# One weight load of a decode kernel, w1, sent as two transfers: 16 rows, then 112

## The chip, the cores and the metric

The kernel runs on one core of a Trainium2 chip. The metric is the device time of one execution in microseconds (us); lower is better. Before the change it is 342.52 us, the median of three runs (342.45 to 342.62).

## What is computed

Two rows x (batch 2, one token each, 512 wide) pass through two branches, mixed by a gate. The reference, cut to what matters:

```python
g = sigmoid((x * gate_w).sum(-1, keepdims=True))
# branch A: attention over a cache, 32 heads of 128, 4096 positions
q = (x @ wq).reshape(2, 1, 32, 128).transpose(0, 2, 1, 3)
p = softmax(einsum("bhqd,bhkd->bhqk", q, k_cache) * 128 ** -0.5)
a = einsum("bhqk,bhkd->bhqd", p, v_cache).transpose(0, 2, 1, 3).reshape(2, 1, 4096) @ wo
# branch B: two dense layers, 512 -> 1376 -> 512
b = maximum(x @ w1, 0) @ w2
out = g * a + (1 - g) * b
```

All tensors are bf16. k_cache and v_cache hold 67 MB each; the weights together some 11 MB. Nearly all that the kernel does is to bring these bytes on chip once.

## The kernel before

On-chip memory has 128 partitions. One large tile, `kv`, holds three regions of 8 MB (NREG = 3, 64 KB on each partition). The k and v caches are cut into eight units of 8 MB each (NU = 8). SyncE (SP) issues one transfer for a unit, into the region that is next in turn; the list `order` fixes the sequence of k and v units by hand. From the fourth unit on, SP first waits until the work on the unit that had the region before has ended (`freed`), so up to three units are in flight or in use.

The third region first serves another end: it holds wq (4 MB), w1 (1.4 MB), x and gate_w, since these are needed only at the start. ScalarE (ACT) issues the loads of x (L233) and gate_w (L234) on its own queue. SP issues w1 (L235) and then wq (L236), then the first two k units (L250). The third k unit needs the region of the weights, and SP waits there for `pe_qh`, `dve_setup` and `act_q`: the projections must have read wq and w1, and q must have been taken out.

On TensorE (PE), `gate()` turns x and forms the gate's sum. Then `x_proj()` forms q (from wq) and the first dense layer (from w1) in one loop of four passes; its matmuls go through the helpers on L314 and L320. Ahead of it PE waits for wq and for w1. A transfer of SP adds 16 to its semaphore when it has landed, so the wait is for 16 on each.

w1 is 512 x 1376. The load views it as 128 rows of four consecutive lines (`"(p t) f -> p (t f)"`), so a partition gets 4 x 1376 x 2 = 11,008 consecutive bytes. There are sixteen DMA engines, and a transfer's rows are dealt out among them.

From there on the units stream: VectorE (DVE) turns each k unit in place (L404), PE multiplies (L314), ACT and DVE form the softmax, GpSimd (POOL) spreads the weights p (L449), and PE multiplies the v units. At the end SP loads w2 (L252) and wo in four pieces (L255); the last matmuls (L598) add both branches into one result, two casts (L623, L625) write it out, and SP sends it (L257).

The instructions of each engine are collected in a list and emitted in two parts: a first few of each (the tuple `rest`; for SP the first four: w1, wq and two k units) ahead of PE's program, the others behind it.

Of the kernel before, what the change touches and what calls it, by code (L numbers as in the profile page):

```python
# [94 lines left out]
def bass_gated_mix__gqa_block_cached__dense_activation_relu__decode_kernel(  # L95
# [61 lines left out]
    w1_sb = kv[:, C, 16384:21888]  # L157
# [16 lines left out]
    def psf(p0, p1, c0, n):  # L174
        return PSF[p0:p1, c0:c0 + n]
# [4 lines left out]
    sem = {n: nc.alloc_semaphore("sem_" + n) for n in names}  # L180
# [16 lines left out]
    def freed(what):  # L197
        kind, u = what
        return f"pesc_{u}" if kind == "k" else f"pe_v_{u}"

    def sp(fn, waits=(), dwaits=()):
        P.add("sp", fn, waits=waits, dwaits=dwaits)
# [4 lines left out]
    def dve(fn, waits=(), signal=None, dwaits=()):  # L207
        P.add("dve", fn, waits=waits, signal=signal, dwaits=dwaits)

    def act(fn, waits=(), signal=None, dwaits=()):  # L210
        P.add("act", fn, waits=waits, signal=signal, dwaits=dwaits)

    def pe(fn, waits=(), signal=None, dwaits=()):
        P.add("pe", fn, waits=waits, signal=signal, dwaits=dwaits)
# [17 lines left out]

    act(lambda e: e.dma_start(x_sb[0:2], A_x.rearrange("b s d -> (b s) d")).then_inc(sem["x"], 16))  # L233
    act(lambda e: e.dma_start(x_sb[2:3], gate_w.rearrange("(o d) -> o d", o=1)).then_inc(sem["gw"], 16))  # L234
    sp(lambda e: e.dma_start(w1_sb, B_w1.rearrange("(p t) f -> p (t f)", t=4)).then_inc(sem["w1"], 16))  # L235
    sp(lambda e: e.dma_start(wq_sb, A_wq.rearrange("(p t) n -> p (t n)", t=4)).then_inc(sem["wq"], 16))  # L236
    for n, what in enumerate(order):
        if n >= NREG:
            waits = [freed(order[n - NREG])]
        else:  # L240
            waits = ["pe_qh", "dve_setup", "act_q"] if n == C else []
        if what == ("v", 7):
            c0 = 0
            for i, k in enumerate(LASTV):
                c1 = c0 + k * 4096
                sp(lambda e, n=n, c0=c0, c1=c1, i=i: e.dma_start(kv[:, n % NREG, c0:c1], unit_in(("v", 7))[:, c0:c1]).then_inc(sem["v7" + "ab"[i]], 16),
                   waits=waits if i == 0 else [])
                c0 = c1
        else:
            sp(lambda e, n=n, what=what: e.dma_start(kv[:, n % NREG, :], unit_in(what)).then_inc(sem_reg[n % NREG], 16),  # L250
               waits=waits)
# [50 lines left out]
    def r_(e, name):  # L302
        if name not in reg:
            reg[name] = e.alloc_register(name)
        return reg[name]

    def by_reg(e, ap, name):
        x = e.lower_ap(ap)
        n = reg[name].name
        return mybir.RegisterAccessPattern(ap=x.ap, dtype=x.dtype, memsetref=x.memsetref, regref=n, is_regloc_offset=False,  # L310
                                           reg_ap_offset=n, const_ap_offset=0, const_sub_tensor_id=0)

    def mm(e, dst, lhsT, rhs, cols=128, at=0, load=True):
        return e.add_instruction(mybir.InstMatmult(  # L314
            name=nc.get_next_instruction_name(), engine=mybir.EngineType.PE, ins=[rhs, lhsT], outs=[e.lower_ap(dst)],
            start_tensor_calc=False, stop_tensor_calc=False, tile_size=(128, cols), tile_position=(0, at),
            bass_skip_group_check=True, ldweights=load))

    def clear(e, dst, n, stop=False):
        return e.matmul(dst, lhsT=nil, rhs=nil.unsqueeze(1).to_broadcast([32, 4, 128]) if n == 512 else nil[:, 0:n],  # L320
                        start=not stop, stop=stop, tile_position=(0, 0), skip_group_check=True)

    def addresses(e, base, offs, first):
        for k, o in enumerate(offs):
            e.reg_add(r_(e, f"a{first + k}"), r_(e, base), o)
# [4 lines left out]
    def enter(name, parent=None, engines=(mybir.EngineType.PE,)):  # L330
        parent = nc.bb_map[parent] if parent else nc.cur_bb
        if open_block:
            open_block.pop().__exit__(None, None, None)
        b = nc.body(name, parent=parent, valid_engines=list(engines))
        b.__enter__()
        open_block.append(b)
# [3 lines left out]
    def x_proj():  # L340
        wqv = wq_sb.rearrange("p (t u a x) -> p t a u x", t=4, u=4, a=4)
        place_of = [(96 + r, 10, 128) for r in range(10)] + [(0, 1, 96)]

        def fn(e):
            for half in range(2):
                clear(e, psf(0, 128, V_C0 + BANK * half, BANK), 512)
            clear(e, psf(0, 128, H_C0, 2 * NF), 2 * NF)
            e.reg_mov(r_(e, "rm"), at["kv"] + 2 * C * REG)
            e.reg_mov(r_(e, "rh"), at["kv"] + 2 * (C * REG + 16384))
            e.reg_mov(r_(e, "rw"), at["zero"] + 4 * 636)  # L350
            e.reg_mov(r_(e, "p"), 0)
            e.br("x_pass")
            enter("x_pass")
            addresses(e, "rm", [2 * (256 * a + 2048 * half) for a in range(4) for half in range(2)], 0)
            addresses(e, "rw", [2 * 31], 8)
            addresses(e, "rh", [2 * (row + (m - 1) * n) for row, n, m in place_of], 9)
            for a in range(4):
                for half in range(2):
                    mm(e, psf(32 * a, 32 * a + 32, V_C0 + BANK * half, BANK), by_reg(e, xT32[:, 0, :], "a8"),
                       by_reg(e, wqv[:, 0, a, 2 * half:2 * half + 2, :], f"a{2 * a + half}"), 32, 32 * a, load=not half)  # L360
            for ft, (row, n, m) in enumerate(place_of):
                mm(e, psf(0, m, H_C0 + 2 * ft, 2), by_reg(e, w1_sb[:, row:row + (m - 1) * n + 1:n], f"a{9 + ft}"),
                   by_reg(e, xT32[:, 0, 0:2], "rw"))
            e.reg_add(reg["rm"], reg["rm"], 2 * 4096)
            e.reg_add(reg["rh"], reg["rh"], 2 * DFF)
            e.reg_add(reg["rw"], reg["rw"], 2 * 32)
            e.reg_add(reg["p"], reg["p"], 1)
            e.br_lt(reg["p"], 4, on_true="x_pass", on_false="x_done")
            enter("x_done")
            return clear(e, psf(0, 128, H_C0, 2), 2, stop=True)  # L370
        pe(fn, dwaits=[(sem["wq"], 16), (sem["w1"], 16)], waits=["act_xT"], signal="pe_qh")
        qt = ptm[:].rearrange("p x c h -> p (x c h)").bitcast(f32)
        dve(lambda v: v.transpose(out=qt.rearrange("p (n q) -> p n q", q=32).rearrange("p (y e) q -> p y e q", e=2),  # L373
                                  in_=PSF[:, V_C0:V_C0 + 1024].rearrange("p (y q e) -> p y e q", q=32, e=2)),
            waits=["pe_qh"], signal="dve_qt")
        act(lambda a: a.activation(out=q_sb[:].rearrange("p b u h k -> p b (u h k)"),
                                   in_=qt.rearrange("p (n x) -> p x n", x=32)[:, 0:2], func=ACT.Copy),
            waits=["dve_qt"], signal="act_q")
# [265 lines left out]
    hint_here()  # L644
    gate()
    x_proj()
    w_block(0)
    w_block(1)
# [48 lines left out]

    P.resolve()

    rest = (("sp", nc.sync, 4), ("act", nc.scalar, 2), ("pool", nc.gpsimd, 4), ("dve", nc.vector, 0))  # L700
    for name, eng, n in rest:
        P.emit(name, eng, 0, n)
    P.emit("pe", nc.tensor)
# [31 lines left out]
```

## Time and profile before

| what | value |
|---|---|
| median of three runs | 342.52 us (342.45 to 342.62) |
| the profiled execution | 342.64 us, of which its span is 341.3 us |
| busy: PE, DVE, POOL, ACT | 209.9, 155.4, 41.8, 13.9 us |
| SP's queue q1: packets, bytes, share of 16 engines | 3460, 145.33 MB, 98.7% |
| mean rate of all transfers | 426 GB/s |
| w1, issue to landing | 1376 KB, 5.8 us |
| wq, issue to landing | 4096 KB, 15.0 us |

The span runs from the first to the last instruction of one profiled execution. A queue's share is the time that its packets took, over sixteen engines and the whole span. A packet is one consecutive piece that one DMA engine moves; for w1 it is one row of 11,008 bytes. In the timeline, a line gives the start, the time, the engine, the source line and the operation; "SPq" and "ACTq" are the instructions by which SP and ACT issue transfers. In the windows, a row gives a stretch, its length, the busy time of PE, PEld (weight loads), DVE, ACT and POOL, then the granted TensorE clock, the DMA share and the rate.

### The profile page before, as it was taken

The numbers are of one execution on the slowest core, as the hardware profiler recorded it, in microseconds if no ns is written. First come the engines' busy times: TensorE is split into PE (matmuls) and PEld (weight loads), VectorE is DVE, ScalarE is ACT, GpSimd is POOL, SyncE is SP. The second block draws the span as 40 slices with busy tenths as digits, with TensorE's granted clock in tenths as the row PEclk, the third lists the DMA queues.
The fourth block names the chain that finished last, engine by engine and source line by source line (L and its number), as shares of the span: only waits on it lengthen the run. The fifth ranks groups of instructions, "written<-read, shape, count | busy, mean of one in ns | idle before, by whom it ended". The sixth has DMA issues, their size and how long they took to land. (4 is left out here: it accounts for less than half of the span.)

```text
span 341.3 us, 3101 instructions
## 1 busy us (share of the span) xinstructions
PE 209.9 (61%) x1243; PEld 33.9 (10%) x843; DVE 155.4 (46%) x45; ACT 13.9 (4%) x37; POOL 41.8 (12%) x53
## 2 busy tenths in 40 slices
PE   0080079685968909972995059820993773718387
PEld 0040011000100101110111001100100100101024
DVE  1010897979799769229800693019805000000111
ACT  2001000000000020000000000000003000000000
POOL 1000000000000004005002300050000235050400
PEclk9999999999898965996799559965696659676789
DMA  8998989898999999998989898989999999999896
GB/s 346 434 492 369 492 369 492 369 492 369 492 392 468 399 461 445 415 484 376 492 369 492 369 492 369 492 369 492 392 468 392 468 438 424 398 441 461 374 440 264
DMA packets 3580, 145.46 MB, mean 426 GB/s; under 512 B 405, under 2 KB 634, under 8 KB 762
## 3 DMA queue, kind: packets, MB, share of 16 engines
q1 hardware_dynamic: 3460, 145.33, 98.7%
q10 hardware_dynamic: 118, 0.10, 0.1%
q8 instruction: 1, 0.02, 0.0%
q14 instruction: 1, 0.01, 0.0%
HBM read 145.43 MB, written 0.00 MB: 426 GB/s over the span
## 5 line engine op out<-in xcount | busy, mean ns | idle before, releaser
L404 DVE STREAM_TRANSPOSE kv<-kv 128x8192 uint32<-128x8192 uint32 (+1 forms) x17 | 138.6, 8186 | 74.4 <-DMA kv<-in_A_k_cache_dram 74.4
L314 PE MATMUL PS<-kv,zero 128*128 (+1 forms) x544 | 130.3, 421 | 40.4 <-PEq L481 40.4
L314 PE MATMUL PS<-kv,ptw 128*32 x512 | 48.1, 469 | 11.7 <-issue 11.5
L320 PE MATMUL PS<-zero 32*128 32x512 bf16 (+2 forms) x21 | 9.7, 537 | 57.6 <-ACT zero L410 20.3
L449 POOL TENSOR_TENSOR ptw<-E,mask 128x512 bf16<-128x512 bf16 x32 | 32.2, 1038 | 21.1 <-PE PS L314 10.9
L467 DVE TENSOR_TENSOR X<-PS,maskc 128x512 f32<-128x512 f32 x2 | 1.4, 692 | 64.1 <-PE PS L314 64.1
L314 PEld LDWEIGHTS PS<-kv,zero 128*128 (+1 forms) x144 | 13.6, 103 | 154.6 <-issue 154.6
L393 POOL TENSOR_TENSOR zero<-q_sb,mask 128x32 bf16<-128x32 bf16 x8 | 1.9, 251 | 147.0 <-PE PS L314 123.3
L471 POOL TENSOR_TENSOR X<-X,maskc 128x512 f32<-128x512 f32 x6 | 6.2, 1039 | 109.2 <-ACT X L470 109.2
L314 PE MATMUL PS<-X,zero 128*64 128x512 f32 x16 | 11.6, 819 | 12.3 <-PEq L481 12.3
L314 PEld LDWEIGHTS PS<-kv,ptw 128*32 x512 | 8.7, 99 | 50.4 <-issue 49.7
L320 PEld LDWEIGHTS PS<-zero 32*128 32x128 bf16 x21 | 2.1, 109 | 69.4 <-issue 43.7
L373 DVE STREAM_TRANSPOSE ptw<-PS 128x1024 f32<-128x1024 f32 x1 | 1.3, 1251 | 16.4 <-PE PS L320 16.4
L415 DVE TENSOR_REDUCE zero<-PS 128x2 f32<-128x2048 f32 x2 | 4.5, 2271 | 9.1 <-PE PS L314 9.1
L470 ACT ACTIVATE X<-PS 128x512 f32<-128x512 f32 x6 | 3.6, 597 | 71.4 <-PE PS L314 71.4
L422 ACT ACTIVATE nrow<-mmax 128x32 f32<-128x32 f32 x2 | 0.5, 228 | 132.8 <-DVE mmax L419 132.8
L440 DVE STREAM_TRANSPOSE E<-E 128x2048 bf16<-128x2048 bf16 x2 | 4.6, 2300 | 2.4 <-ACT E L430 2.4
L410 ACT ACTIVATE zero<-zero 1x1 f32<-1x1 f32 x9 | 1.8, 200 | 84.9 <-DMA kv<-in_A_v_cache_dram 67.9
L430 ACT ACTIVATE E<-PS,negm 128x1024 bf16<-128x1024 f32 x4 | 4.4, 1109 | 0.6 <-DVE negm L426 0.6
L284 PE MATMUL PS<-kv 3*128 3x3 bf16 x4 | 0.3, 165 | 6.5 <-DMA kv<-in_gate_w_dram 6.5
L598 PE MATMUL PS<-kv,oW 128*2 128x256 bf16 x64 | 4.0, 272 | 0.4 <-DMA kv<-in_A_wo_dram 0.4
L314 PEld LDWEIGHTS PS<-X,zero 128*64 (+1 forms) x16 | 1.8, 161 | 15.8 <-issue 15.6
(49 smaller groups left out, 27.6 us busy)
## 6 DMA issues: line engine op xcount, KB each, us to landing
kv<-in_A_v_cache_dram SPq DMA_DIRECT2D x1, 6144.0 KB, 36.7
kv<-in_A_wq_dram SPq DMA_DIRECT2D x1, 4096.0 KB, 15.0
kv<-in_A_wo_dram SPq DMA_DIRECT2D x1, 2560.0 KB, 35.9
kv<-in_A_v_cache_dram SPq DMA_DIRECT2D x1, 2048.0 KB, 41.3
kv<-in_B_w_dram SPq DMA_DIRECT2D x1, 1376.0 KB, 5.8
kv<-in_B_w_dram SPq DMA_DIRECT2D x1, 1280.0 KB, 30.1
kv<-in_A_wo_dram SPq DMA_DIRECT2D x1, 1024.0 KB, 37.9
kv<-in_A_wo_dram SPq DMA_DIRECT2D x1, 384.0 KB, 38.4
```

Source lines behind the costliest of these rows:

```text
L314: return e.add_instruction(mybir.InstMatmult(name=nc.get_next_instruction_name(), engine=mybir.EngineType.PE, ins=[rhs, lhsT], outs=[e.low ...
L320: return e.matmul(dst, lhsT=nil, rhs=nil.unsqueeze(1).to_broadcast([32, 4, 128]) if n == 512 else nil[:, 0:n], start=not stop, stop=stop, ...
L393: pool(lambda g: g.tensor_tensor(out=out, in0=q, in1=msk, op=ALU.mult), waits=([["act_q", "dve_mask8"], []] + [[f"pesc_{x}"] for x in rang ...
L404: ins = v.transpose(out=reg[:, 4096 * p0:4096 * p1], in_=reg[:, 4096 * p0:4096 * p1])
L410: return lambda a: a.activation(out=tick[:, 2 + i:3 + i], in_=tick[:, 0:1], func=ACT.Copy).then_inc(sem["go"], n)
L415: dve(lambda v: v.tensor_reduce(out=mpad[:, 0:2], in_=PSF[:, 0:2048].rearrange("p (x h q) -> p h x q", h=2, q=16), axis=AX.XY, op=ALU.max) ...
L430: act(lambda a, h=h: a.activation(out=E[:].rearrange("p (x h q) -> p h x q", h=2, q=16)[:, h], in_=PSF[:, 0:2048].rearrange("p (x h q) -> ...
L440: dve(lambda v: v.transpose(out=E[:], in_=E[:]), waits=[f"act_exp{b}"], signal=f"dve_et{b}")
L449: pool(lambda g, src=src, dst=dst: g.tensor_tensor(out=dst, in0=src, in1=msk, op=ALU.mult), waits=(([f"dve_et{b}"] if ub == 0 else []) + ( ...
L470: act(lambda e: e.activation(out=X2[:], in_=src, func=ACT.Copy), waits=[f"pe_v_{v}"], signal=f"act_x_{v}")
L471: pool(lambda e: e.tensor_tensor(out=X, in0=X, in1=msk, op=ALU.mult).then_inc(sem["xg"], 1), waits=[f"act_x_{v}"] + ([] if v else ["dve_se ...
L598: pe(lambda e, g=g: e.matmul(psf(64 * g, 64 * g + 2, FIN_C0, 256), lhsT=w, rhs=m[:, 256 * g:256 * g + 256], start=start, stop=stop, tile_p ...
```

## The change

w1 is loaded by two transfers on the same queue: the first sixteen rows (partitions 0 to 15), then rows 16 to 127. Both add 16 to the same semaphore, and PE waits for 32. SP's first part of the program has five instructions instead of four. Nothing else differs.

```diff
-    sp(lambda e: e.dma_start(w1_sb, B_w1.rearrange("(p t) f -> p (t f)", t=4)).then_inc(sem["w1"], 16))
+
+    for p0, p1 in ((0, 16), (16, 128)):
+        sp(lambda e, p0=p0, p1=p1: e.dma_start(w1_sb[p0:p1], B_w1.rearrange("(p t) f -> p (t f)", t=4)[p0:p1]).then_inc(sem["w1"], 16))
     sp(lambda e: e.dma_start(wq_sb, A_wq.rearrange("(p t) n -> p (t n)", t=4)).then_inc(sem["wq"], 16))
...
-        pe(fn, dwaits=[(sem["wq"], 16), (sem["w1"], 16)], waits=["act_xT"], signal="pe_qh")
+        pe(fn, dwaits=[(sem["wq"], 16), (sem["w1"], 32)], waits=["act_xT"], signal="pe_qh")
...
-    rest = (("sp", nc.sync, 4), ("act", nc.scalar, 2), ("pool", nc.gpsimd, 4), ("dve", nc.vector, 0))
+    rest = (("sp", nc.sync, 5), ("act", nc.scalar, 2), ("pool", nc.gpsimd, 4), ("dve", nc.vector, 0))
```

## The prediction

> **What bounds the kernel now.** I read the busy shares first, then the DMA queues, then the chain that ended last, and then the first microseconds in small windows. The page's second and third parts:
>
> ```profile
> DMA  8998989898999999998989898989999999999896
> GB/s 346 434 492 369 492 369 492 369 492 369 492 392 468 399 461 445 415 484 376 492 369 492 369 492 369 492 369 492 392 468 392 468 438 424 398 441 461 374 440 264
> ...
> q1 hardware_dynamic: 3460, 145.33, 98.7%
> ```
>
> No compute engine passes 61% (PE, 209.9 us of 341.3); SP's queue q1 keeps sixteen DMA engines occupied for 98.7% of the span. Nothing in the middle is slack: 145.33 MB in 0.987 x 341.3 = 336.9 us is 431 GB/s, and every slice stands near it except the first (346) and the last (264). So **the end is where the DMA stream ends**, and a shift of the stream's start moves the end by as much, undiminished. The end itself, from the timeline:
>
> ```profile
> 339.05 0.37 PEld L598 LDWEIGHTS PS<-kv,oW 128*2 128x2 bf16 x8 [0.28 <-DMA kv<-in_A_wo_dram]
> 339.69 0.38 ACT L625 ACTIVATE ptw<-PS 2x256 bf16<-2x256 f32 x1 [5.21 <-PE PS L598]
> 339.69 0.41 DVE L623 CAST ptw<-PS 2x256 bf16<-2x256 f32 x1 [5.82 <-PE PS L598]
> 340.13 0.33 SPq L257 DMA_DIRECT2D out_dram<-ptw  x1
> ```
>
> The last matmuls wait for the last pieces of wo, and only the casts and the 2 KB output follow. The slowest of the sixteen engines decides, since each landing needs all of them.
>
> The change sits at the other end. The timeline of the first 3 us, then the windows (length, five engines' busy time, granted clock, DMA share, GB/s):
>
> ```profile
> 0.74 0.40 SPq L235 DMA_DIRECT2D kv<-in_B_w_dram  x1
> 0.74 0.54 ACTq L233 DMA_DIRECT2D kv<-in_A_x_dram  x1
> ...
> 1.19 0.42 SPq L236 DMA_DIRECT2D kv<-in_A_wq_dram  x1
> 1.31 0.23 ACTq L234 DMA_DIRECT2D kv<-in_gate_w_dram  x1
> ...
> 1.65 1.16 SPq L250 DMA_DIRECT2D kv<-in_A_k_cache_dram  x2
> ```
> ```profile
> 1.00:1.50 0.50, 0.00 (x0) 0.00 (x0) 0.00 (x0) 0.00 (x0) 0.33 (x2) 1.00 0.00 0
> 1.50:2.00 0.50, 0.00 (x0) 0.00 (x0) 0.00 (x0) 0.00 (x0) 0.50 (x1) 1.00 1.16 180
> 2.00:2.50 0.50, 0.00 (x0) 0.00 (x0) 0.08 (x1) 0.03 (x1) 0.39 (x1) 1.00 0.61 154
> 2.50:3.00 0.50, 0.00 (x0) 0.00 (x0) 0.50 (x4) 0.50 (x1) 0.00 (x0) 1.00 0.34 132
> 3.00:3.50 0.50, 0.00 (x0) 0.00 (x0) 0.50 (x3) 0.50 (x1) 0.00 (x0) 1.00 1.14 484
> ```
>
> w1 is issued at 0.74 us; nothing moves before 1.5; then for 1.5 us the stream runs at 132 to 180 GB/s before it reaches its rate. The windows book a packet's bytes where it starts. The packet records behind these rows say the same: w1 is 128 packets of 11,008 bytes, eight to an engine. The first packet of each engine starts between 1.77 and 2.73 us and takes 0.41 to 1.36 us, 0.92 on the mean; the later ones take 0.413 us (26.65 GB/s an engine). This **ramp** is what the change touches.
>
> **The change part by part.**
>
> *It removes* nothing: same bytes, same packets.
>
> *It adds* one DMA instruction on SP, and turns the first transfer into sixteen rows (16 x 11,008 = 176 KB, one packet an engine) and the second into 112 rows (seven an engine). That a few rows do go one to an engine is seen on x, whose two rows are two overlapping packets of 1,024 bytes.
>
> (a) *An earlier first byte.* x (two rows, ACT's queue) and w1 (128 rows) are both issued at 0.74; x's packets start at 1.67, w1's first at 1.77: a shorter transfer starts 0.10 us earlier. The output's two rows are issued at 340.13 and start at 340.89, 0.76 us later, against 1.03 us for w1: 0.27 earlier. Nothing excludes zero. Bounds 0 to -0.27; I take **-0.10**, the pair issued at the same moment.
>
> (b) *A later second transfer.* SP's steps in the timeline are 0.74, 1.19, 1.65: one instruction more costs 0.45 us. So seven eighths of w1 become available 0.45 us later, while the first packet feeds an engine for 0.41 us. Balance **+0.04**. If SP's added step were as short as the output's issue (0.33, and the same 0.05 between), it would be 0.38 and the balance -0.03. wq and the k regions are issued 0.45 later as well, which costs nothing: w1 still occupies the engines until about 6.5 us (0.74 + its 5.8 to landing), 4.8 us after k's first issue at 1.65. If that cover were gone, it would cost the whole 0.45.
>
> (c) *Sixteen neighbouring rows at once.* In the trace every long transfer spreads sixteen engines over all 128 partitions. The new first transfer aims all sixteen at partitions 0 to 15. No row shows that. The one near row is x: two engines writing partitions 0 and 1 at the same time took 44 ns each, against 46 for a packet of that size elsewhere, so no sharing; but that is 2 KB, little enough to be taken up on the way, and not 176 KB. If n engines share a way into neighbouring partitions, a packet takes n x 0.413: bounds n = 1 (cost 0, x's pair) and n = 16 (cost 6.2). I take the geometric middle, n = 4: 1.65 instead of 0.41, **+1.24**. A hidden part would need idle DMA time behind it, and the page has none. [...]
>
> (d) *112 rows in sevens.* 128 rows run at 0.413 us a packet; sevens that begin at row 16 need not keep the engines apart as eights do. Bounds 0 (w1's own rate) and +2.89 (each of seven packets at double time). I take **0**, the nearest row, and keep the upper end for the range.
>
> *It moves* PE's wait on w1 from a count of 16 to 32. PE waits there for wq too, issued at 1.19 with 15.0 us to landing, so about 16.2; the first matmul of x_proj starts at 16.28, when w1 has been there nearly 10 us. Queued behind that wait is all of PE's projection, and behind it q and the issue of the third k region, at 26.4; but the two regions issued before it still fill the engines for 16.8 MB / 426 GB/s = 39 us after 16. Cost 0.
>
> **Sum:** -0.10 + 0.04 + 1.24 + 0 = **+1.18 us**. The profiled execution took 342.64 us, its span 341.3 and 1.3 around it; it would become 343.8. That run is 0.12 above the median of three, 342.52, so the forecast is **343.7 us**.
>
> **The rivals.**
>
> *Nothing moves.* If x's pair is the right row for (c), -0.10 + 0.04 = -0.06: **342.5**. For it: the step (0.45) and the packet (0.41) are almost equal, so the first transfer only fills the time until the second arrives. Against: it needs sixteen writers side by side to run as freely as two. [...]
>
> *The ramp goes away: faster.* From 1.67 (x's first packet) to 3.5 the windows book 0.5 x (180 + 154 + 132 + 484) = 475 KB; at 427 GB/s it would be 781 KB. The missing 306 KB are 0.72 us. If the ramp is the price of preparing eight packets an engine before any flows, and the short transfer escapes it as x's did, with the second ready in time, the gain is 0.72 + 0.10: **341.7**. With the larger lead it is 0.99, 341.5. For it: x shows no slow packet. Against: (b), the second transfer comes 0.45 us later and would show its own ramp.
>
> *The ramp is paid twice: slower, by another way.* An engine with one packet has nothing queued behind it; if the second transfer starts cold again, its first packet costs 0.92 instead of 0.41 on the mean, 1.36 on the worst engine: +0.51 to +0.95. With (a) and (b), +0.45 to +0.89, middle **343.2**. It decides from the point where the first packet ends before the second transfer's packets are ready. Against: if the first packet is itself slow, the second start is hidden behind it.
>
> That the change does not do what it says (the sixteen rows on fewer than sixteen engines) would put several packets in a row on some engines; four each is the same 1.24 late on those, so its time is the forecast's, and I count it there.
>
> **How the numbers follow.** Neighbouring rows share a way: 0.38, 343.2 to 344.9 (n = 3, +0.77, up to n = 4 with a part of (d)). Ramp twice: 0.12. Nothing moves: 0.30, 342.2 to 342.9. Ramp gone: 0.20, 341.5 to 342.2. A measurement of this kernel tells about 0.2%, 0.69 us, from no change: slower holds nearly all of the first case and most of the second, 0.46; faster holds most of the last, 0.17; the rest, 0.37, is within. For eight in ten the range reaches from the middle of the faster case to the first case's upper end, 341.8 to 344.9, and leaves out half of the faster case and the part of (c) and (d) above n = 4.
>
> **What would show it.** In the packet records, w1's first sixteen packets: about 1.65 us each, or several ends in steps of 0.41, bears (c) out; 0.41 from 1.7 on refutes it. The packets of the 112 rows at 0.413 bear out (d); longer ones among them would price it. First packets of the second transfer near 0.92 mean the second ramp. The issue of wq should move from 1.19 to about 1.64, the first matmul of x_proj (16.28) and the last wo landing (339.05) by the same amount as the end. If the windows after 4 us show a rate other than now, or the first matmul moves and the end does not, the view that the stream carries its start to the end is wrong, and with it every step here.

## The result and the profile after

The changed kernel takes 344.71 us (median of six runs, 344.51 to 345.35) against 342.57 for the kernel before beside it (342.45 to 342.74): 2.14 us slower, ratio 1.0063, 95% interval 1.0052 to 1.0074. The forecast was 343.7 with a range of 341.8 to 344.9. The sign held; the loss is 1.8 times the forecast's 1.18 us, and the larger part of it comes from a term that the sum had put at nothing.

The page after, its second and third parts:

```profile
DMA  7999898989899998989898999989898989899896
GB/s 226 451 466 474 382 481 374 489 367 489 367 489 397 458 474 382 489 367 489 367 489 367 489 412 443 481 374 489 367 489 367 489 367 491 372 462 458 370 437 265
...
q1 hardware_dynamic: 3476, 145.33, 98.7%
```

The share is the same 98.7%, though less was moved per microsecond (145.33 MB in a span of 343.2 us instead of 341.3): an engine that is held up in a packet counts as occupied. The sixteen packets more are of 4 bytes each (402 of that size instead of 386), and the kernel has one transfer more; w1 itself is still 128 packets of 11,008 bytes. The first slice fell from 346 to 226 GB/s; that is the place of the loss. The timeline's start, SP's issues alone:

```profile
0.74 0.85 SPq L237 DMA_DIRECT2D kv<-in_B_w_dram  x2
1.64 0.49 SPq L238 DMA_DIRECT2D kv<-in_A_wq_dram  x1
2.16 1.00 SPq L252 DMA_DIRECT2D kv<-in_A_k_cache_dram  x2
```

wq is issued at 1.64 instead of 1.19, as foreseen. The same windows as before, and on to 7 us (the columns are as above; the last three are the granted clock, the DMA share and GB/s):

```profile
1.50:2.00 0.50, 0.00 (x0) 0.00 (x0) 0.00 (x0) 0.00 (x0) 0.50 (x1) 1.00 1.05 310
2.00:2.50 0.50, 0.00 (x0) 0.00 (x0) 0.08 (x1) 0.03 (x1) 0.39 (x1) 1.00 0.57 114
2.50:3.00 0.50, 0.00 (x0) 0.00 (x0) 0.50 (x4) 0.50 (x1) 0.00 (x0) 1.00 1.58 264
3.00:3.50 0.50, 0.00 (x0) 0.00 (x0) 0.50 (x3) 0.50 (x1) 0.00 (x0) 1.00 0.38 88
...
4.00:5.00 1.00, 0.40 (x8) 0.23 (x6) 0.00 (x0) 0.44 (x3) 0.00 (x0) 1.00 1.06 330
5.00:6.00 1.00, 0.00 (x0) 0.00 (x0) 0.17 (x1) 0.33 (x2) 0.00 (x0) 1.00 1.09 308
6.00:7.00 1.00, 0.00 (x0) 0.00 (x0) 0.00 (x0) 0.00 (x0) 0.00 (x0) 1.00 0.95 253
```

The kernel before has, from 4 us:

```profile
4.00:5.00 1.00, 0.00 (x0) 0.00 (x0) 0.00 (x0) 0.00 (x0) 0.00 (x0) 1.00 0.91 385
5.00:6.00 1.00, 0.00 (x0) 0.00 (x0) 0.00 (x0) 0.00 (x0) 0.00 (x0) 1.00 1.49 637
6.00:7.00 1.00, 0.26 (x4) 0.20 (x4) 0.00 (x0) 0.17 (x1) 0.00 (x0) 1.00 0.69 295
```

More packets start before 2.0 (310 against 180), so the first transfer does get moving sooner. But where the kernel before books 385, 637 and 295 between 4 and 7 us, 439 on the mean (the 637 holds the first large packets of wq, booked where they start), this one books 330, 308 and 253, 297 on the mean, with the DMA share near 1: the engines are occupied and slow. The packet records show it packet by packet. Mean time of w1's packets, in sets of sixteen in the order of their start, and of wq's first sixteen behind them (us):

```
            w1, 11,008 bytes each                            wq first
before      0.91 0.42 0.41 0.41 0.41 0.42 0.42 0.41          1.21
after       0.59 1.03 0.62 0.59 0.55 0.61 0.69 0.63          1.44
```

The end moved with it. The changed kernel's timeline:

```profile
18.30 1.02 PE L322 MATMUL PS<-zero 32*128 32x512 bf16 x3 [13.62 <-DMA kv<-in_A_wq_dram]
...
340.94 0.37 PEld L600 LDWEIGHTS PS<-kv,oW 128*2 128x2 bf16 x8 [0.25 <-DMA kv<-in_A_wo_dram]
...
342.02 0.32 SPq L259 DMA_DIRECT2D out_dram<-ptw  x1
```

The last wait for wo ends 1.89 us later (339.05 to 340.94), as does the output's issue (340.13 to 342.02); the first matmul of x_proj moved from 16.28 to 18.30, by 2.02; the profiled executions differ by 344.51 - 342.64 = 1.87. What is lost in the first eight microseconds reaches the end whole, within 0.2 us.

### The profile page after: what moved, and what is told of

The parts are those of the page before. It is cut to its first block, busy times and chain, and to the rows that moved or that the text cites. A ratio compares the mean times of both kernels' runs of the same rounds, so it can differ in the third digit from the quotient of the medians.

```text
span 343.2 us, 3102 instructions
## 1 busy us (share of the span) xinstructions
PE 211.0 (61%) x1243; PEld 33.9 (10%) x843; DVE 155.4 (45%) x45; ACT 13.9 (4%) x37; POOL 41.8 (12%) x53
## 3 DMA queue, kind: packets, MB, share of 16 engines
q1 hardware_dynamic: 3476, 145.33, 98.7%
## 5 line engine op out<-in xcount | busy, mean ns | idle before, releaser
L316 PE MATMUL PS<-kv,zero 128*128 (+1 forms) x544 | 131.9, 425 | 39.2 <-PEq L483 39.2
L316 PEld LDWEIGHTS PS<-zero,kv 128*128 (+1 forms) x44 | 3.0, 158 | 3.5 <-issue 3.5
L316 PE MATMUL PS<-zero,kv 128*128 (+1 forms) x44 | 3.3, 200 | 0.0
```

What stands on the lines that cost most here:

```text
L316: return e.add_instruction(mybir.InstMatmult(name=nc.get_next_instruction_name(), engine=mybir.EngineType.PE, ins=[rhs, lhsT], outs=[e.low ...
```

## The experiments

Theory A: engines meet at the destination. Each DMA engine writes a share of the rows, and when a transfer does not cover all 128 partitions, several engines would write through the same way (entrance) into on-chip memory and wait for each other; it would hold for the 112 rows above all. A way is an assumption: it is not seen in any record, only what rows cost that are thought to share one. Theory B: two transfers would cost more than one, by a second cold start. Theory C is A for the sixteen rows: sixteen neighbouring rows would share ways by fours, the four being the forecast's estimate. Each kernel starts from the kernel before; differences are between medians of runs made side by side. The cuts of code show the load alone; the counts that PE waits for, and SP's first part of the program, follow it.

**e1: both transfers with all 128 rows, split by columns.**

```diff
+    for c0, c1 in ((0, 688), (688, 5504)):
+        sp(... e.dma_start(w1_sb[:, c0:c1], B_w1.rearrange("(p t) f -> p (t f)", t=4)[:, c0:c1]) ...)
```

> w1 in two transfers of all 128 rows each: the first 1,376 bytes of every row (176 KB, as much as the sixteen rows held), then the other 9,632. If the loss comes from how 112 rows are dealt to the engines (theory A), it is gone: between 0.3 us faster and 0.3 slower than the kernel before, with packets of 9,632 bytes at about 0.36 us. If it comes from sending two transfers, with a second cold start (theory B), the second transfer's first packets are again about 0.6 us too long and the time is 0.6 to 1.9 us above the kernel before.

342.80 against 342.69, ratio 1.0006 (0.9997 to 1.0016): no difference. The packets of 9,632 bytes run at 0.36 us, and its windows show the full rate between 4 and 6 us:

```profile
4.00:5.00 1.00, 0.27 (x4) 0.18 (x4) 0.17 (x1) 0.43 (x3) 0.00 (x0) 1.00 0.98 414
5.00:6.00 1.00, 0.00 (x0) 0.00 (x0) 0.00 (x0) 0.15 (x1) 0.00 (x0) 1.00 1.05 441
```

So the second transfer, SP's added issue and a slow second start (the first sixteen of its large packets take 0.80 us on the mean, 0.36 being full rate) cost together nothing that these runs can tell from zero (-0.10 to +0.55 us). B, which asked for 0.6 at least, falls. The small first transfer brings no gain either. Why the slow second start costs nothing is not shown; that it falls into time which the stream loses at its start anyway would fit.

**e2: 112 rows first, then sixteen.**

```diff
+    for p0, p1 in ((16, 128), (0, 16)):
```

> Rows 16 to 127 first, rows 0 to 15 behind them. Theory A (sevens): the 112 packets after the first of each engine stay at 0.55 to 0.69 us instead of 0.41 although nothing stands ahead of them, and the time is 1.5 to 2.2 us above the kernel before. Theory B (second cold start): the 112 packets run at 0.41, the sixteen show the slow start, at most 0.6 us above. Theory C (sixteen neighbouring rows share a way): the sixteen packets take about 1.65 us each and cost 1.2.

345.76 against 342.69, 3.07 us slower (1.0086, 1.0069 to 1.0103): more than any one theory said, and what A (1.5 to 2.2) and C (1.2) come to together. After their slow start the packets of the 112 rows keep to means of 0.50 to 0.71 us, as A has it with nothing ahead of them. The packets of about 1.65 us that C foretold do not show: the last sixteen of w1 take 0.82. But wq's first packets behind them take 2.11 us instead of 1.21. The two excesses, 0.41 and 0.90, make 1.31 us, near the price of C; I read the second as the same writes, booked one packet later. Here, in mid-stream, the whole price shows.

**e3: two halves.**

```diff
+    for p0, p1 in ((0, 64), (64, 128)):
```

> Rows 0 to 63, then 64 to 127: four rows an engine. Theory A in the form 'engines meet when the rows a transfer covers are fewer than all 128': packets at up to 0.83 us, 3.3 us above the kernel before at most; in the form 'only odd shares such as sevens make them meet': 0.41 us and no loss. Theory B: 0.6 us above.

345.75 against 342.69, 3.06 us slower (1.0086, 1.0069 to 1.0102). Its packets settle at 0.85 us, twice 0.413, and the stream at half rate:

```profile
4.00:5.00 1.00, 0.00 (x0) 0.00 (x0) 0.00 (x0) 0.00 (x0) 0.00 (x0) 1.00 0.97 199
5.00:6.00 1.00, 0.00 (x0) 0.00 (x0) 0.00 (x0) 0.00 (x0) 0.00 (x0) 1.00 1.09 253
6.00:7.00 1.00, 0.32 (x6) 0.27 (x6) 0.00 (x0) 0.19 (x1) 0.00 (x0) 1.00 1.10 231
7.00:8.00 1.00, 0.22 (x4) 0.13 (x4) 0.17 (x1) 0.48 (x3) 0.00 (x0) 1.00 0.91 187
```

In this run half of the partitions gave about half of the rate (187 to 253 GB/s from 4 to 8 us, where e1 has 414 and 441 from 4 to 6), with even shares (four rows an engine) too.

**e4: sixteen rows once more ahead of the whole w1**, into spare bytes of the same region (`spare`, behind x's columns of `kv`).

```diff
+    sp(... e.dma_start(spare[0:16], B_w1.rearrange("(p t) f -> p (t f)", t=4)[0:16]) ...)
     sp(... w1 as before ...)
```

> The kernel before, with rows 0 to 15 of w1 read once more ahead of it, into spare bytes of partitions 0 to 15; w1 itself stays whole, and PE waits for both. This adds one packet an engine, 0.41 us at full rate. If the narrow transfer costs nothing beyond its bytes, 0.3 to 0.5 us above the kernel before. If sixteen neighbouring rows share ways by fours (theory C), its bytes need 1.65 us, part of which passes while the stream would only be starting: 1.0 to 1.7 us above, and the packets behind it, not its own, are long.

343.74 against 342.62, 1.12 us slower (1.0032, 1.0022 to 1.0042). The added bytes are worth 0.41, so the narrow transfer costs about 0.7 at the head of the stream, not 1.24. The 0.7 is a middle and no level that was measured: the ten runs fall in two groups of five, at 343.4 and at 344.0 to 344.4, with the median between them, and the interval gives 0.3 to 1.0. That the missing part is hidden in the start is argued, not shown. The packets behind it are long, not its own (0.53, then 1.05), as C has it; a second slow start would look alike here, and only e1 says that it costs no more than 0.55.

**e5: 112 rows once more behind w1**, with e10, all 128 rows at the same place, as control, and e11 with rows 32 to 127.

```diff
     sp(... w1 as before ...)
+    sp(... e.dma_start(spare[16:128], B_w1.rearrange("(p t) f -> p (t f)", t=4)[16:128]) ...)
```

> The kernel before, with a transfer of rows 16 to 127 of w1 once more, into spare bytes of the same region, behind w1 and ahead of wq; PE waits for it too. This adds 7 packets an engine in the middle of a running stream. Theory A: packets at about 0.62 us, so 4.3 us more than the kernel before, and up to 0.3 on top from the first packets behind it. Theory B: no cold start in a running stream, packets at 0.413, 2.9 us more.

> Control for the added 112 rows: all 128 rows of w1 once more into the spare bytes. At full rate 8 packets of 0.413, 3.3 us above the kernel before, less than the 4.2 that 112 rows cost, though it moves more.

> Rows 32 to 127 once more into the spare bytes, six an engine. At full rate 2.5 us above the kernel before. If any share other than eight makes engines meet, 3.3 to 4.5; if only odd shares do, 2.5.

| added rows | bytes at full rate | measured | ratio and interval |
|---|---|---|---|
| 128 (e10) | 8 x 0.413 = 3.30 us | +3.29 (345.88 against 342.59) | 1.0095 (1.0078 to 1.0112) |
| 112 (e5) | 7 x 0.413 = 2.89 us | +4.24 (346.93 against 342.69) | 1.0130 (1.0113 to 1.0147) |
| 96 (e11) | 6 x 0.413 = 2.48 us | +4.85 (347.44 against 342.59) | 1.0142 (1.0125 to 1.0158) |

In these runs fewer rows than 128 took longer. The control meets its bytes to 0.01 us; 112 rows lose 1.35 and 96 lose 2.37, with a time of 4.85 beyond the 4.5 that I had put as the upper end. That only odd shares do it is refuted: sixes lose too. Whether 96 rows take longer than 112 the times do not settle, since their intervals overlap; the packets of the added 96 rows do take longer, 0.68 to 0.75 us in the sets behind the first against 0.52 to 0.64. The windows from 7 us, e10 first, then e11:

```profile
7.00:8.00 1.00, 0.27 (x4) 0.18 (x4) 0.11 (x1) 0.47 (x3) 0.00 (x0) 1.00 0.88 374
8.00:9.00 1.00, 0.00 (x0) 0.00 (x0) 0.05 (x1) 0.20 (x1) 0.00 (x0) 1.00 1.24 528
```
```profile
7.00:8.00 1.00, 0.50 (x8) 0.33 (x8) 0.00 (x0) 0.36 (x2) 0.00 (x0) 1.00 0.98 242
8.00:9.00 1.00, 0.00 (x0) 0.00 (x0) 0.17 (x1) 0.41 (x2) 0.00 (x0) 1.00 1.17 275
```

A DMA share near 1 at 242 GB/s: again occupied and slow.

**e6: w1 in eight transfers of sixteen rows.**

```diff
+    for p0, p1 in tuple((p, p + 16) for p in range(0, 128, 16)):
```

> w1 in eight transfers of sixteen neighbouring rows each. Without theory C the packets stay at 0.41 us and the loss is at most what SP's seven more issues at 0.45 us bring, 3.2 us spread over a stream that needs 3.3: 0 to 0.6 us. By theory C each transfer runs at a quarter: 9.9 us above the kernel before if the engines stay in step, about 3.3 if they drift apart so that two transfers overlap.

349.59 against 342.62, 6.97 us slower (1.0199, 1.0182 to 1.0217). The packets settle at 1.37 us, 3.3 times 0.413, between the two forms of C: neither full step nor two transfers side by side. Whether the engines drift apart by that much is not seen in the records.

**e8 and e9: the same sixteen rows to neighbouring and to distant partitions.** Both read the same 320 KB of wq behind w1, into spare bytes.

```diff
+    sp(... e.dma_start(spare[0:16],    wq rows 0 to 15, 20,480 bytes each) ...)     # e8
+    sp(... e.dma_start(spare[0:128:8], the same) ...)                                # e9
```

> The kernel before, with one more transfer behind w1 in the running stream: sixteen rows of wq, 20,480 bytes each, into spare bytes of the neighbouring partitions 0 to 15. At full rate a packet takes 0.77 us, so 0.8 us above the kernel before. By theory C with four on a way, 3.06 us, so 3.1 above.

> The same sixteen rows of wq at the same place in the stream, but into every eighth partition (0, 8, ... 120). Same reads, same bytes, other destinations. If what costs is the reads, or the smallness of the transfer, the time equals that of the neighbouring partitions. If it is the destination (theory C), it is 0.8 us above the kernel before, or 1.5 if two of these partitions still share a way.

Neighbours: 345.87 against 342.62, +3.25 us (1.0092, 1.0073 to 1.0111). Every eighth partition: 344.26, +1.64 (1.0048, 1.0030 to 1.0065). At full rate both would be +0.77; the ratios to that are 4.2 and 2.1. Both came out as theory C had them (3.1 and 1.5 above). The reads are the same, so in this pair it is the destination that costs. The ratios fit the fours of theory C for the neighbours and twos for the spread rows; what it is at the destination that costs, no run shows. For the transfers of 64, 96 and 112 rows no run separates destination and source in this way; that the same cause holds there is argued from this pair. The windows, e8 first:

```profile
7.00:8.00 1.00, 0.00 (x0) 0.00 (x0) 0.17 (x1) 0.56 (x3) 0.00 (x0) 1.00 0.92 197
8.00:9.00 1.00, 0.00 (x0) 0.00 (x0) 0.00 (x0) 0.00 (x0) 0.00 (x0) 1.00 0.89 229
```
```profile
7.00:8.00 1.00, 0.00 (x0) 0.00 (x0) 0.17 (x1) 0.58 (x3) 0.00 (x0) 1.00 0.95 328
8.00:9.00 1.00, 0.00 (x0) 0.00 (x0) 0.00 (x0) 0.00 (x0) 0.00 (x0) 1.00 1.22 524
```

**e7: the same split on wq instead of w1.**

```diff
+    for p0, p1 in ((0, 16), (16, 128)):
+        sp(... e.dma_start(wq_sb[p0:p1], A_wq.rearrange("(p t) n -> p (t n)", t=4)[p0:p1]) ...)
```

> w1 whole; wq instead is sent as rows 0 to 15 and rows 16 to 127, with rows of 32,768 bytes, 2.98 times those of w1. If the loss is shared ways, it grows with the bytes: 2.98 times the 2.14 us of the change, 6.4 us above the kernel before (5 to 7.5). If it is a fixed price of two transfers or of their shape, 2 us above.

352.91 against 342.59, 10.32 us slower (1.0295, 1.0278 to 1.0312): no fixed price, but also more than in proportion to the bytes (6.4), and beyond the 5 to 7.5 that I had expected. Its windows from 12 to 24 us stand at 262 GB/s, two of them here:

```profile
14.00:16.00 2.00, 0.00 (x0) 0.00 (x0) 0.00 (x0) 0.00 (x0) 0.00 (x0) 1.00 0.88 262
16.00:18.00 2.00, 0.00 (x0) 0.00 (x0) 0.00 (x0) 0.00 (x0) 0.00 (x0) 1.00 0.97 262
```

e8 and e5 allow part of the surplus: by estimate, the sixteen rows in mid-stream cost 3 x 1.213 = 3.64 beyond their bytes (e8's ratio of 4.2, taken as four), and sevens at e5's price are 1.35 x 2.98 = 4.02, together 7.7. The last 2.7 us are not settled. The packets say where to look: the median of wq's is 2.16 us against 1.213, 1.8 times as long, and w1's behind the first two sets of the changed kernel about 1.5 times (0.62 against 0.413). So the long rows lost more by sevens here than the short ones; why is open.

## Why the prediction was right in sign and short in size

- **What bounds the kernel**: held. The loss at the start (wq's last packet ends at 17.65 instead of 15.82, 1.83 us later) is the loss at the end (1.89), within 0.1 us.
- **(a) the earlier first byte**, -0.10: w1's first packet starts at 1.77 us in both kernels, so the lead itself is 0. What is true is another thing: the sixteen first packets end 0.50 us earlier on the mean (2.51 against 3.01), 0.32 of it because they are shorter, 0.59 instead of 0.91, and the rest because they start closer together. In e1, whose first packets also end early and whose second transfer has a slow start of its own, no such gain is left.
- **(b) the step**, +0.04: wq's issue moved by exactly 0.45, and e1 puts the whole of (a), (b) and a second start at +0.11 us (-0.1 to +0.55 by its interval).
- **(c) sixteen neighbouring rows**, +1.24: that neighbouring rows cost more is right, and so is the price of n = 4 (e8: 4.2 times; e9, spread out: 2.1); the shared way behind it is not shown. The forecast's n = 4 was only the middle of two bounds, so that it hit is luck. The size is too large at this place: "A hidden part would need idle DMA time behind it, and the page has none" is the sentence that failed. The slow start may be such time; e4 measures 0.7 (0.3 to 1.0). The packet times that I had named as the sign (about 1.65 us each) did not show either. The sets take 0.59, then 1.03, against 0.91 and 0.42, and e4, with a whole w1 behind the sixteen rows, shows the same 0.53 and 1.05: I read this as held-up writes that stand on the packets behind.
- **(d) 112 rows in sevens**, 0: this is the term that failed. I took the row that looked nearest, w1's own 128 rows, and kept +2.89 only for the range. e5 against e10 measures +1.35 (about 1.0 to 2.1 by e5's interval). The changed kernel's own packets say the same: from the third set on they take 0.55 to 0.69 us, where e4's, with 128 rows, are back at 0.41 to 0.47. These six sets lose 1.21 us against the kernel before, and wq's first packets 0.23, together 1.44.
- With both put right, 0.7 + 1.35 + about 0.1 = 2.15 against 2.14 measured. The terms come from different kernels, and with intervals 0.7 and 1.2 us wide that they meet to 0.01 is luck; the size is support, not proof. The forecast's 343.7 owed something to luck as well: (c) was about 0.5 too large and (d) 1.35 too small, and the result lies inside the range, 0.2 below its end, because a part of (d) had been left in it.
- **The rivals**: a second cold start is visible (0.80 us for e1's second transfer) and costs nothing that e1 can tell from zero; "the ramp goes away" happened by a third and was lost again; "nothing moves" needed sixteen writers side by side to run as freely as x's pair of 1,024 bytes (44 ns each), and e8's sixteen did not (4.2 times the full-rate time). Two halves of the partitions, e3, gained nothing and cost 3.06 us.

## What to carry to other kernels

In a stream that keeps the DMA engines occupied as this one does, do not count a load's time by its bytes alone: every part of w1 or wq that went to fewer than 128 partitions here ran below the full rate, and a shorter transfer took longer than a whole one (112 rows 4.2 us, 128 rows 3.3). In e8 and e9 the destination of the rows decided (4.2 and 2.1 times the full-rate time); for the other transfers that is argued, not shown. If such a load must be split, split its columns and keep all partitions; here that cost nothing measurable (+0.11 us, -0.10 to +0.55), and gained nothing. A high DMA share showed here that engines were occupied, not that they moved bytes at their rate (0.98 at 242 GB/s in e11): read it beside the GB/s.

## What was not expected of the hardware

A held-up packet seems to be booked late. In e8 the sixteen packets to neighbouring partitions show 1.83 us, and the packets behind them, which belong to a transfer to all 128 partitions, 2.38 instead of 1.21; the two excesses, 1.06 and 1.17, make 2.2 of the 2.48 us that this run lost beyond its bytes (3.25 - 0.77). So the record of one packet did not say which transfer was slow; the sum with the packets behind it came near. And 96 rows lost by the medians more than 112, and not less as one would expect of fewer bytes (2.37 us, 1.8 to 2.9, against 1.35, 1.0 to 2.1; the intervals just overlap). A part of this can be argued, though no run shows it. Suppose that leaving out 16 or 32 neighbouring rows makes none of the other rows faster. Then by this estimate 112 and 96 rows still need 8 x 0.413 = 3.30 us, as long as 128 rows (e10: 3.29). What they lost beyond that, 0.94 and 1.55 us, stays open: which partitions an engine gets in such shares is not seen in the records.
